# Counting whole turns of an angle in the low half of a float's word, with a new order of all operations

## The chip, the cores and the metric

The kernel runs on one core of one Trainium2 chip. The metric is the device time of one execution in microseconds. Three runs of the kernel before took 470.22, 471.32 and 486.15 us, so its time is the median, 471.32 us. The core has five engines that run side by side: PE (matmuls; PEld are its weight loads), DVE, ACT and POOL (elementwise work), and SP, which here only issues DMA transfers.

## The reference

A recurrence over 768 time steps feeds a small mixture of attention experts. The first part keeps a complex 48x48 state for each of 4 batches and 8 heads; each step multiplies row d of the state by a complex number of modulus at most 0.999 and adds `k v`:

```
mag = np.sqrt(a_re * a_re + a_im * a_im)
scale = np.minimum(mag, 0.999) / (mag + 1e-06)
a_re_n, a_im_n = (a_re * scale, a_im * scale)
for t in range(S):
    new_re = ar * S_re - ai * S_im
    new_im = ar * S_im + ai * S_re
    S_re, S_im = (new_re + kv, new_im)
    y[:, :, t] = np.einsum('bhd,bhde->bhe', q[:, :, t], S_re)
```

The second part takes `y` (4 x 768 x 384) as `x`. A gate `x @ w_gate` picks two of four experts for each token; each expert is causal attention with 64-wide projections, and the two outputs are summed with the gate's weights:

```
logits = x @ w_gate
q, k, v = x @ wq[e], x @ wk[e], x @ wv[e]
a = softmax(causal(scale * (q @ k.transpose(0, 2, 1))))
ye = a @ v @ wo[e]
out += mask[..., None] * w[:, :, kk:kk + 1] * ye
```

## The kernel before, in words

**The recurrence becomes matmuls.** The product of the complex factors up to step t is a modulus times a turn by an angle, so the kernel takes the logarithm of each modulus and the angle of each factor (`quotients`, `magnitudes`, `arcs`), sums both over time (scans on DVE), and multiplies `q` and `k` by the exponentials and by sine and cosine (`products`). With these, a chunk of 128 steps is plain linear attention: `head` transposes `k` on PE into tile pk and forms the scores psc, `state` adds a chunk's contribution pu to the running state tst, and `tail` adds the part within the chunk and the part from the state in tile yu, whose two halves (a rounded one and the rest) become `x`. In the trace a matmul on plain 32-bit floats stands as two instructions where the program has one.

**The angles** are the part that the change rewrites (function `angles`, lines 527 to 544). [...]

- "turns": `Bi` is scaled from radians to turns (ACT in batch 0, POOL in batches 1 to 3);
- the scan sums `Bi` along time into `A` (DVE);
- "wrap": `MAGIC`, 1.5 times two to the 23rd, is added to `A`, which rounds it to a whole number (POOL in all batches);
- a SCALAR_TENSOR_TENSOR on DVE takes `MAGIC` off again and subtracts `A`;
- "fold": the absolute value (ACT), for the cosine;
- `sines` takes both sines with a scale of minus 2 pi (ACT).

**Layout and stages.** The 384 rows (8 heads x 48) of a batch lie in three tiles j of 128 partitions (ab for the factors, qk for q and k). `regroup` sends them by DMA into tiles fm, one for each of four pairs of heads g, with 96 partitions. For g = 2 and 3 of batch 0 these have names of their own (fm2, fm3). Time is cut into three blocks k of 256 steps. Batch 0 is prepared in parts (`PARTS`): first j 0 at block 0, then j 1 and 2 at block 0, then blocks 1 and 2. Batch b + 1 is prepared while batch b is in the second part. For g = 3 the result yu goes to a tile yt and from there by six small DMAs into the three tiles x; every projection (tiles pp and pv) of a batch reads all three.

**What sets the order.** No engine order is found when the program is built. Every operation is recorded (4415 of them) and then issued in the order of a table, `ORDER`; each engine runs its own operations strictly in that order. A second table, `ROOMS`, picks the buffers. A third, `WARM`, puts matmuls on constants (tile src, line 380, 128x512 in bf16; their result, warm, is never read) on PE ahead of chosen operations: 242 in all, 151 of them at the start, 35 behind the first block of batch 0. All other instructions carry line 387.

Of the kernel before, what the change touches and what calls it, by code (L numbers as in the profile page):

```python
# [13 lines left out]
I32 = mybir.dt.int32  # L14
U8 = mybir.dt.uint8
AF = mybir.ActivationFunctionType
# [14 lines left out]
TWO_PI = 6.2831845  # L31
# [359 lines left out]
def attention_moe(ctx: ExitStack, tc: tile.TileContext, ak, vk, w, out):  # L391
# [154 lines left out]
    def sines(b, j, k0, k1):  # L546
        A, Bi, X, Y, Q, K, G, G2 = views(b, j, k0, k1)
        act(Bi, Bi, AF.Sin, scale=-TWO_PI)
        act(A, A, AF.Sin, scale=-TWO_PI, bias=halfpi)

# [413 lines left out]
```

## Time and profile before

| | |
|---|---|
| median of three runs | 471.32 us |
| the profiled execution, its time | 474.05 us |
| the profiled execution, its span from the first to the last instruction | 472.3 us |
| PE busy, share of the span | 453.0 us, 96% |
| DVE, ACT, POOL busy | 335.7, 328.7, 236.0 us |
| mean granted clock of PE | 0.949 of full speed |
| matmuls on constants, busy time on PE | 58.5 us, 242 of them |

The profiled execution is 2.73 us above the median. A busy PE isn't PE at its peak: in some stretches the throttle grants it half of its 2.4 GHz, and the same matmuls then take twice as long. The column PEclk of the tables by stretch shows this.

### The profile page before, as it was taken

Reading aid. Unit: us, or ns where it says so; the run is one execution under the profiler, and the core shown is the slowest. Engines: PE = TensorE matmul, PEld = TensorE weight load, DVE = VectorE, ACT = ScalarE, POOL = GpSimd, SP = SyncE. Lnnn points to the kernel's source line nnn. Section 1 sums busy time; section 2 is a strip of 40 time slices with the busy share of each in tenths; the row PEclk is TensorE's granted clock in tenths of the full one; section 3 lists DMA queues with packets and bytes.
Section 4 is the critical chain, followed back from the end, with each engine's and each line's share of the span. In section 5 each row is a group of like instructions: output and inputs, shape, how many; then the busy total and the mean of one; then the engine's idle time right before and its main releaser. Section 6 shows DMA issues by size and latency. Waiting matters only on the chain.

```text
span 472.3 us, 9992 instructions
## 1 busy us (share of the span) xinstructions
PE 453.0 (96%) x3754; PEld 350.8 (74%) x3754; DVE 335.7 (71%) x768; ACT 328.7 (70%) x731; POOL 236.0 (50%) x214
## 2 busy tenths in 40 slices
PE   8998999999998999998999999999999999999896
PEld 3447868778686678867988877788798787887565
DVE  3977548778789899774999895878965543666622
ACT  6984387976559979876789988768755565324453
POOL 4264054544424689587235697394224518003780
PEclk9997599979969999999999999999959999999999
DMA  7905067702973562365085813580445111100102
GB/s 274 348 3 134 1 160 198 207 19 77 237 206 67 168 194 78 87 176 158 4 199 129 234 46 102 117 236 18 76 112 139 30 25 29 51 18 17 52 1 101
DMA packets 22239, 53.46 MB, mean 113 GB/s; under 512 B 3216, under 2 KB 9456, under 8 KB 22064
## 3 DMA queue, kind: packets, MB, share of 16 engines
q1 hardware_dynamic: 22192, 52.83, 40.9%
q8 instruction: 29, 0.48, 0.4%
q14 instruction: 18, 0.15, 0.1%
HBM read 26.74 MB, written 4.72 MB: 67 GB/s over the span
## 4 chain that ended last, share of the span: by engine, by line
PE 58%; ACT 15%; DMA 9%; DVE 5%; POOL 5%; SPq 4%; issue 3%; POOLq 0%; ACTq 0%; DVEq 0%
PE pp L387 8%; PE psc L387 8%; PE yu L387 7%; PE psS L387 7%; PE pw L387 5%; ACT qk L387 5%; PE pv L387 5%; PE pu L387 5%; DMA fm<-qk 4%; ACT ab L387 4%; PE po L387 4%; SPq L387 4%; PE pm L387 3%; PE pk L387 3%; DMA ab<-in_ak_dram 3%
## 5 line engine op out<-in xcount | busy, mean ns | idle before, releaser
L387 POOL TENSOR_TENSOR pe<-pe 128x512 f32<-128x512 f32 (+1 forms) x64 | 83.9, 1311 | 16.7 <-PE po L387 13.3
L387 ACT ACTIVATE pe<-psS 128x512 f32<-128x512 f32 (+2 forms) x96 | 47.9, 540 | 22.2 <-PE psS L387 19.3
L387 ACT ACTIVATE ab<-ab 128x768 f32<-128x768 f32 (+2 forms) x81 | 55.6, 695 | 9.3 <-DVE ab L387 5.3
L387 PE MATMUL psc<-fm 96*128 96x128 f32 x384 | 60.5, 312 | 1.1 <-DVE sum L387 0.4
L380 PE MATMUL warm<-src 128*128 128x512 bf16 x242 | 58.5, 397 | 1.4 <-POOL src L387 1.4
L387 ACT ACTIVATE qk<-qk 128x768 f32<-128x768 f32 (+5 forms) x105 | 57.4, 563 | 1.1 <-DVE qk L387 0.7
L387 PEld LDWEIGHTS psc<-fm 96*128 96x128 f32 x384 | 54.4, 220 | 3.9 <-issue 0.9
L387 DVE CUSTOM_DVE_ANT_0 pm<-pm,mask 128x384 f32<-128x384 f32 (+4 forms) x96 | 47.2, 511 | 12.3 <-PE pm L387 11.8
L387 POOL TENSOR_SCALAR_AFFINE_SELECT pe<-pe 128x256 f32<-128x256 f32 x48 | 22.7, 485 | 63.6 <-ACT pe L387 31.3
L387 POOL TENSOR_TENSOR qk<-qk 128x768 f32<-128x768 f32 (+2 forms) x24 | 36.7, 1542 | 32.8 <-ACT qk L387 30.8
L387 PE MATMUL pp<-x,whi 128*128 128x256 f32 (+1 forms) x216 | 46.6, 328 | 3.6 <-ACT ob L387 2.0
L387 POOL TENSOR_TENSOR qk<-qk,ab 128x768 f32<-128x768 f32 (+2 forms) x19 | 28.7, 1510 | 39.4 <-ACT ab L387 20.9
L387 PE MATMUL psS<-qka 64*128 64x256 f32 (+3 forms) x480 | 47.4, 304 | 0.3
L380 PEld LDWEIGHTS <-src 128*128 128x128 bf16 x242 | 23.6, 102 | 31.0 <-issue 6.1
L387 ACT ACTIVATE tst<-sum,fm 96x48 f32<-96x48 f32 x128 | 38.3, 326 | 11.3 <-DVE sum L387 11.1
L387 DVE TENSOR_TENSOR pts<-psc,keep 128x512 f32<-128x512 f32 x48 | 32.8, 683 | 17.5 <-PE psc L387 15.3
L387 DVE TENSOR_TENSOR qk<-qk,ab 128x768 f32<-128x768 f32 (+2 forms) x41 | 38.5, 960 | 9.3 <-ACT ab L387 8.0
L387 PE MATMUL po<-pe,v 128*64 128x256 f32 (+3 forms) x320 | 44.3, 395 | 0.0
L387 PEld LDWEIGHTS psS<-qka 64*128 64x128 f32 x480 | 36.9, 185 | 7.7 <-issue 3.6
L387 PE MATMUL yu<-pts,vt 128*64 128x128 f32 x384 | 41.0, 309 | 0.4
L387 POOL TENSOR_SCALAR ab<-ab 128x768 f32<-128x768 f32 (+2 forms) x24 | 22.3, 931 | 37.0 <-DVE ab L387 19.0
L387 PEld LDWEIGHTS pp<-x,whi 128*128 128x128 f32 x216 | 33.2, 188 | 9.7 <-ACT ob L387 2.2
(106 smaller groups left out, 984.8 us busy)
## 6 DMA issues: line engine op xcount, KB each, us to landing
fm<-qk SPq DMA_DIRECT2D x18, 578.2 KB, 7.6
ab<-in_ak_dram SPq DMA_DIRECT2D x9, 768.0 KB, 7.2
qk<-in_ak_dram SPq DMA_DIRECT2D x9, 768.0 KB, 5.0
vt<-in_vk_dram SPq DMA_DIRECT2D x16, 384.0 KB, 8.4
out_dram<-ob SPq DMA_DIRECT2D x24, 192.0 KB, 1.9
fm<-qk SPq DMA_DIRECT2D x10, 385.5 KB
fm<-qk SPq DMA_DIRECT2D x16, 192.8 KB, 3.8
x<-yt SPq DMA_DIRECT2D x72, 32.0 KB, 2.0
```

Source lines behind the costliest of these rows:

```text
L380: chain("tensor", nc.tensor.matmul(x, *map(real, self.warm), start=True, stop=True))
L387: chain(engine, getattr(getattr(nc, engine), method)(*map(real, a), **{x: real(y) for x, y in k.items()}))
```

## The change

It has two parts. The first is in `angles` and `sines`. The angle stays in radians through the scan, so the operation "turns" is gone (15 of them: 6 on ACT in batch 0, 9 on POOL later). "Wrap" now multiplies the running angle by 1 / (2 pi) and adds `MAGIC` in one operation; in batch 0 it moves from POOL to ACT, 6 operations. After that addition the low 16 bits of the float's word hold the whole number of turns, and DVE reads them as 16-bit integers, every second one, multiplies by minus 2 pi and adds the angle. The result is within half a turn in radians, and both sines need hardly a scale.

```
-        if ENG0["turns"][k0][j] == "a" if b == 0 else ENG["turns"] == "a":
-            act(Bi, Bi, AF.Copy, scale=0.5 / math.pi)
-        else:
-            e("turns").tensor_scalar(Bi, Bi, 0.5 / math.pi, 0.0, op0=OP.mult, op1=OP.add)
         n = (k1 - k0) * C2
         nc.vector.tensor_tensor_scan(A, ones.to_broadcast([128, n]), Bi, carry[b, j] if k0 else 0.0, op0=OP.mult, op1=OP.add)
...
-        e("wrap").tensor_scalar(Bi, A, 1.0, MAGIC, op0=OP.mult, op1=OP.add)
-        nc.vector.scalar_tensor_tensor(Bi, Bi, MAGIC, A, op0=OP.subtract, op1=OP.subtract)
+
+        if (ENG0["wrap"][k0][j] if b == 0 else ENG["wrap"]) == "a":
+            act(Bi, A, AF.Copy, scale=0.5 / math.pi, bias=MAGIC)
+        else:
+            e("wrap").tensor_scalar(Bi, A, 0.5 / math.pi, MAGIC, op0=OP.mult, op1=OP.add)
+        nc.vector.scalar_tensor_tensor(Bi, Bi.bitcast(I16)[:, ::2], -TWO_PI, A, op0=OP.mult, op1=OP.add)
...
-        act(Bi, Bi, AF.Sin, scale=-TWO_PI)
-        act(A, A, AF.Sin, scale=-TWO_PI, bias=halfpi)
+        act(Bi, Bi, AF.Sin, scale=NEAR_ONE)
+        act(A, A, AF.Sin, scale=-NEAR_ONE, bias=halfpi)
...
-        "turns": ("aaa", "aaa", "aaa"), "wrap": ("ppp", "ppp", "ppp"), "fold": ("aaa", "aaa", "aaa")}
+        "wrap": ("aaa", "aaa", "aaa"), "fold": ("aaa", "aaa", "aaa")}
```

The second part is new tables: `ORDER` (4400 operations), `ROOMS`, and `WARM`, which now holds 205 matmuls on constants in place of 242 (the number stands second in each entry):

```
-    72: ("psu_4", 151), 1080: ("psu_4", 35), 390: ("psa_1", 8), 410: ("psu_4", 2), 420: ("psa_0", 3), 540: ("psu_4", 2), 1147: ("psa_2", 11),
-    1287: ("psa_2", 5), 1180: ("psa_2", 3), 840: ("psu_2", 4), 843: ("psu_1", 4), 1298: ("psu_4", 1), 1345: ("psa_1", 5), 1406: ("psu_0", 2),
-    4381: ("psa_1", 3), 4387: ("psa_1", 3),
+    71: ("psu_4", 146), 1234: ("psu_4", 18), 354: ("psa_2", 1), 1245: ("psa_2", 11), 693: ("psa_2", 2), 779: ("psu_3", 6), 1304: ("psu_2", 5),
+    1336: ("psu_0", 9), 4366: ("psa_0", 4), 4372: ("psa_0", 3),
```

The tables move instructions on every engine; three places matter here. The first is POOL at the start, in the preparation of block 0 of batch 0, where the row TENSOR_SCALAR on ab is "wrap" and TENSOR_TENSOR of qk with ab is `products`. Before:

```order
L387 TENSOR_TENSOR qk<-qk 128x256
L387 TENSOR_TENSOR qk<-qk 128x2x256
L387 TENSOR_SCALAR ab<-ab 128x256 x2
L387 TENSOR_TENSOR qk<-qk,ab 128x256 x2
L387 TENSOR_SCALAR ab<-ab 128x256
L387 TENSOR_TENSOR qk<-qk,ab 128x256 x2
```

And now:

```order
L387 TENSOR_TENSOR ab<-ab 128x512 x2
L387 TENSOR_TENSOR qk<-qk 128x256 x3
L387 TENSOR_TENSOR qk<-qk,ab 128x256 x4
L387 TENSOR_SCALAR qk<-qk 128x2x256
L387 TENSOR_TENSOR qk<-qk,ab 128x256
```

The three "wrap" rows are gone from POOL, and the products follow each other. The second place is PE at the end of block 0 of batch 0. Before, fm_423 is the tile of g = 2 and fm_466 that of g = 3:

```order
L387 MATMUL psc<-fm_466 128x128 x4
L387 MATMUL yu<-pts,vt 64x128 x4
L387 MATMUL yu<-fm_423,tst 48x128 x2
L387 MATMUL pu<-vt,kts 96x48 x4
L387 MATMUL yu<-pts,vt 64x128 x4
L387 MATMUL yu<-fm_466,tst 48x128 x2
L380 LDWEIGHTS src
```

Now fm_252 is g = 2 and fm_426 is g = 3:

```order
L387 MATMUL psc<-fm_426 128x128 x4
L387 MATMUL pu<-vt,kts 96x48 x4
L387 MATMUL yu<-pts,vt 64x128 x4
L387 MATMUL yu<-fm_426,tst 48x128 x2
L387 MATMUL pu<-vt,kts 96x48 x4
L387 MATMUL yu<-pts,vt 64x128 x4
L387 MATMUL yu<-fm_252,tst 48x128 x2
L380 LDWEIGHTS src
```

The yu of g = 3, whose result goes to x by DMA, now stands ahead of pu and yu of g = 2, and not last. Behind it stood 35 matmuls on constants, and now 18. On SP the six transfers x<-yt now follow each other; before, a load of qk stood between the fourth and the fifth. The third place is DVE in batch 2, where the three products of tile j = 1 of batch 3 (qk with ab, 128x3x256) stand among the row maxima (pm, mx) and residues (qka) of batch 2. Before:

```order
L387 ISA pm,mx<-pm,mask 128x384
L387 ISA mx 128x1
L387 TENSOR_TENSOR qka<-pp,qka 128x256
L387 TENSOR_TENSOR qk<-qk,ab 128x3x256 x3
L387 TENSOR_REDUCE mx<-pm 128x1
L387 ISA pm,mx<-pm,mask 128x384
```

And now:

```order
L387 ISA pm,mx<-pm,mask 128x128
L387 ISA mx 128x1
L387 TENSOR_TENSOR qk<-qk,ab 128x3x256
L387 TENSOR_TENSOR ot<-r,ot 128x256
L387 TENSOR_TENSOR qk<-qk,ab 128x3x256
L387 TENSOR_TENSOR sum<-tst,pu 96x96
L387 TENSOR_TENSOR qka<-pp,qka 128x256 x4
L387 TENSOR_TENSOR qk<-qk,ab 128x3x256
```

Two of the three now stand ahead of four residues and behind another row maximum.

## Rows read from the trace of the kernel before

**Rows 1.** The page, part 1: busy us (share of the span) x instructions.

```profile
PE 453.0 (96%) x3754; PEld 350.8 (74%) x3754; DVE 335.7 (71%) x768; ACT 328.7 (70%) x731; POOL 236.0 (50%) x214
```

**Rows 2.** Table by stretch: start:end, length, PE, PEld, DVE, ACT, POOL busy, PEclk, DMA.

```profile
38.00:58.40 20.40, 19.94 (x129) 17.87 (x130) 14.16 (x23) 6.76 (x20) 5.22 (x5) 0.56 0.23 57
58.40:67.00 8.60, 8.60 (x38) 3.71 (x36) 5.86 (x8) 7.57 (x20) 4.64 (x4) 0.86 0.48 126
80.60:98.20 17.60, 16.52 (x158) 12.86 (x157) 14.41 (x35) 17.05 (x40) 7.41 (x5) 1.00 0.61 182
98.20:105.20 7.00, 6.99 (x36) 5.94 (x36) 4.47 (x14) 5.17 (x9) 5.08 (x4) 0.51 0.12 25
129.00:139.20 10.20, 10.20 (x62) 9.43 (x61) 8.06 (x19) 6.18 (x15) 2.91 (x2) 0.50 0.87 243
344.00:354.40 10.40, 10.40 (x66) 9.62 (x64) 6.48 (x19) 5.67 (x15) 2.49 (x1) 0.51 0.45 112
```

**Rows 3.** PE in time, 28 to 39 us: start, us, what, idle before it.

```profile
27.69 8.80 PE L380 MATMUL warm<-src 128*128 128x512 bf16 x40
38.18 0.27 PE L387 MATMUL pk<-ident,fm 96*128 96x96 f32 x1 [1.69 <-DMA fm<-qk]
38.73 0.47 PE L387 MATMUL pk<-ident,fm 96*128 96x96 f32 x3 [0.28 <-DMA fm<-qk]
```

**Rows 4.** ACT in time, at 11 and 27 us.

```profile
11.15 0.61 ACT L387 ACTIVATE qk<-ab 128x512 f32<-128x512 f32 x1
11.67 0.40 ACT L387 ACTIVATE ab<-ab 128x256 f32<-128x256 f32 x1
...
27.18 1.28 ACT L385 ACT_TABLE_LOAD   x1
```

**Rows 5.** DVE, POOL and SP in time, 29 to 35 us.

```profile
29.37 0.69 DVE L387 TENSOR_TENSOR_SCAN ab<-col,ab 128x256 f32<-128x256 f32 x1 [1.39 <-ACT ab L387]
...
30.15 0.49 POOL L387 TENSOR_SCALAR ab<-ab 128x256 f32<-128x256 f32 x1 [1.22 <-DVE ab L387]
...
34.64 1.34 SPq L387 DMA_DIRECT2D fm<-qk  x2
```

**Rows 6.** PE and SP in time, 55 to 67 us.

```profile
55.44 1.52 PE L387 MATMUL pu<-vt,kts 128*96 128x48 f32 x8
...
58.37 8.90 PE L380 MATMUL warm<-src 128*128 128x512 bf16 x35
66.92 0.47 PE L387 MATMUL pv<-whi,x 128*128 128x260 f32 x1
...
59.38 2.57 SPq L387 DMA_DIRECT2D x<-yt  x4
62.00 0.58 SPq L387 DMA_DIRECT2D qk<-in_ak_dram  x1
62.63 1.22 SPq L387 DMA_DIRECT2D x<-yt  x2
```

**Rows 7.** The page, part 6: transfers, KB each, median us from issue to landing.

```profile
x<-yt SPq DMA_DIRECT2D x72, 32.0 KB, 2.0
```

**Rows 8.** Groups by form, whole span: count, busy us, mean ns, idle before.

```profile
L387 POOL TENSOR_SCALAR ab<-ab 128x768 f32<-128x768 f32 x18 | 18.4, 1028 | 24.2 <-ACT ab L387 14.5 <-DVE ab L387 7.3 <-DVE lg L387 1.9
L387 DVE SCALAR_TENSOR_TENSOR ab<-ab 128x768 f32<-128x768 f32 x9 | 9.1, 1017 | 1.2 <-POOL ab L387 1.2
```

**Rows 9.** DVE and PE in time, at 333 and 343 us.

```profile
332.76 2.69 DVE L387 TENSOR_TENSOR qk<-qk,ab 128x768 f32<-128x768 f32 x3
...
342.64 0.47 PE L387 MATMUL pk<-ident,fm 96*128 96x96 f32 x3 [1.16 <-DMA fm<-qk]
```

**Rows 10.** PE in time, 78 to 95 us.

```profile
80.66 0.55 PE L387 MATMUL pk<-ident,fm 96*128 96x96 f32 x4
...
86.88 0.83 PE L387 MATMUL pk<-ident,fm 96*128 96x96 f32 x4
...
94.29 0.60 PE L380 MATMUL warm<-src 128*128 128x512 bf16 x2
```

More of the change, by code (lines that the diff above doesn't have):

```diff
@@ L14 @@
 I32 = mybir.dt.int32
+I16 = mybir.dt.int16
 U8 = mybir.dt.uint8
@@ L30 @@
 MAGIC = 1.5 * 2.0 ** 23
-TWO_PI = 6.2831845
+TWO_PI = 2.0 * math.pi
+NEAR_ONE = 1.0 - 2.0 ** -23
 NEG = -1.0e9
@@ L47 @@
 ORDER = [
[184 rows of a table removed]
[183 rows of a table added]
 ]
 ROOMS = [
[22 rows of a table removed]
[22 rows of a table added]
 ]
 WARM = {
-    72: ("psu_4", 151), 1080: ("psu_4", 35), 390: ("psa_1", 8), 410: ("psu_4", 2), 420: ("psa_0", 3), 540: ("psu_4", 2), 1147: ("psa_2", 11),
-    1287: ("psa_2", 5), 1180: ("psa_2", 3), 840: ("psu_2", 4), 843: ("psu_1", 4), 1298: ("psu_4", 1), 1345: ("psa_1", 5), 1406: ("psu_0", 2),
-    4381: ("psa_1", 3), 4387: ("psa_1", 3),
+    71: ("psu_4", 146), 1234: ("psu_4", 18), 354: ("psa_2", 1), 1245: ("psa_2", 11), 693: ("psa_2", 2), 779: ("psu_3", 6), 1304: ("psu_2", 5),
+    1336: ("psu_0", 9), 4366: ("psa_0", 4), 4372: ("psa_0", 3),
 }
 ENG = {"inv_m": "d", "exp_q": "p", "kts": "a", "xh": "a", "pp": "a", "pv": "a", "first": "p", "inv_a": "p",
-       "exp_k": "p", "q_sin": "d", "k_sin": "p", "q_cos": "d", "k_cos": "d", "turns": "p", "wrap": "p", "fold": "a",
+       "exp_k": "p", "q_sin": "d", "k_sin": "p", "q_cos": "d", "k_cos": "d", "wrap": "p", "fold": "a",
        "sum": "p", "oth": "a", "otl": "d"}
```

411 rows, old and new, of tables (ORDER, ROOMS) are left out of this document.

## The prediction

> **What bounds the kernel now.** I read the page's table of engines first: PE is busy for 453.0 of 472.3 us [rows 1], DVE, ACT and POOL for 50 to 71%. So an operation that leaves POOL or ACT gives nothing by itself; it counts only where PE waits for it or fills a wait with matmuls on constants. The 3754 PE instructions hold 242 of these, 58.5 us, and with 19.3 us of idle time that is what an order can win, besides the clock.
>
> Next comes the table by stretch, for the clock [rows 2]. Four stretches run at the lower of the two levels, 1.2 GHz: most of 38 to 61 us (0.56, then 0.86 for the stretch in which it rises), 98.2 to 105.2, 129 to 139.2 and 344 to 354.4, together about 21 + 7 + 10 + 10 = 48 us. PE is never idle in them, so each costs about half its length. All hold the small matmuls of the recurrence (pk, psc, pu, yu). The reader is to see that busy time hides this loss.
>
> Then the waits and the time-ordered views. At the start PE runs constants until 36.49, waits 1.69 and 0.28 us for the first tile fm, and falls to half clock about 2 us later [rows 3]. Behind block 0, 35 constants bridge the way of yt into x [rows 6]. Until 342.64 PE waits 1.16 us for an fm tile of batch 3 [rows 9], and the clock falls some 1.5 us later.
>
> The profiled execution took 474.05 us, 472.3 of span and 1.75 around it, 2.73 us or 0.6% above the median of 471.32. I make the sum against the former and take the difference off the latter.
>
> **The change part by part.**
>
> *The angles by themselves: nothing.* 9 "turns" leave POOL at about 1.03 us [rows 8], 9.2 us; 6 "wraps" of 0.5 to 0.8 us leave it too. ACT in batch 0 loses 6 operations and gains 6 of the same shapes. PE's work covers all of it; POOL is idle half the span. Without that cover, a turn and a handoff on the way to each fm tile, some 1 us, would count, as at the start.
>
> *The 16-bit, every-second read.* No row shows one. The nearest is the same instruction on 32-bit floats, 1.017 us at 128x768 [rows 8]. From below, 16 bits could not save more than the 0.5 us that half of it is, from above I allow as much again. Fifteen of them lie beside PE work, three on the way to the first tile: 0, ends of minus and plus 0.2 us (half of 0.40 us, its time at 128x256).
>
> *The first fm tile: minus 1.4 us.* Ahead of the sine table's load on ACT, at 27.18, stand two 512-wide operations and one tiny copy fewer than before. One takes 0.52 us from start to start [rows 4], so 1.1 us. On the way from the arc to the scan one operation, 0.3 us, is gone. The "wrap" (0.49 us on POOL [rows 5]) becomes one of about 0.4 on ACT without a handoff to POOL and back. From the scan (29.37) to the transfer's issue (34.64) it takes 5.27 us; going through the new order by hand I get 4.1. So the tile comes between 1.1 and 2.4 us earlier. The 5 fewer constants make 5 x 0.216 (8.80 us less the last one's 0.38, over 39 steps [rows 3]) = 1.1 us. I take 1.1 + 0.3, nearest the smaller end, because the later one of tile and constants sets the start; ends minus 1.1 and minus 2.4.
>
> *The end of block 0: minus 3.1 us.* PE ends the block at 58.37, and six transfers with a load between them leave SP until 63.85; with 2.0 us to land [rows 6, 7] x is there at 65.9, and the projection starts at 66.92. In the new order, yu of g = 3 stands ahead of pu and yu of g = 2, which take 58.37 - 55.44 = 2.9 us at half clock, and the load (0.58) is behind the transfers. So x is there 65.9 - 58.37 - 2.9 - 0.6 = 4.0 us after the block's end. Of the 35 constants, some 7 ran at half clock in the first 3.0 us; 18 would take 3.0 + 11 x 0.216 = 5.4 us where 35 took 8.55. That is 3.1 less, and x still comes first. Ends: 0, if x comes late all the same, and minus 4.5 if the clock is up and x itself sets the start. The next fm tiles are issued behind these six transfers, so they gain as much and the gain isn't given back there.
>
> *The other constants: minus 2.5 us.* From there to the middle of batch 0's attention stood 50, and now 34; at the end 6, and now 7. 15 x 0.216 = 3.2 us if the data are there, 0 if each becomes a wait. I take most of it, as the tiles come 4.5 us earlier and PE reaches them as much earlier.
>
> *Batch 3's tile j = 1: minus 0.6 us.* Its three products start at 332.76, behind a row maximum that waits for PE, and end 335.45; the transfers are issued at once, and PE waits for them from 341.48 [rows 9]. Now two products stand ahead of four residues and the third behind them. This may close the wait of 1.16 us or not; I take half. If it goes, the tile j = 2, whose products come later on the same engine, is the next that can be late.
>
> Sum: -1.4 - 3.1 - 2.5 - 0.6 = -7.6 us: 466.4 against the 474.05, **463.7 us** against the median.
>
> **A rule against it.** The clock stayed up from 80.6 to 98.2 us although pk, psc, pu and yu fill that stretch; 7 constants stand inside it and 8 right ahead of it [rows 2, 10], and the fall came 4 us after the last two. At the start and in batch 3 the falls come about 2 us after the first rows of pk that follow a wait [rows 3, 9]. So in this trace transposes and their company go with falls, constants with a held clock. The Trainium skill, page "TensorE: Matmul & The Clock Gate", Part 4, says that a transpose doesn't count as busy PE time in the same way and doesn't bring the full clock. The trace agrees where it shows falls, but not that every pk costs the clock. By that rule the new order, with one constant in that stretch for 15, would lose the clock there, which is the second rival below.
>
> **The rivals.**
>
> 1. *The half clock shrinks too: 455 us, between the two cases below, chance 0.25.* If the wait at 341.48 closes, the stretch of 10.4 us behind it may go, 5.2 us, and the rest of the wait, 0.6: 463.7 - 5.8 = 458. A second of these stretches (10.2 or 7.0 us [rows 2]) gives 3.5 to 5.1 more, 453 to 454. For it: two of four falls follow a wait for fm. Against: the others don't, and the first stretch, the longest, has the same matmuls in the same density as before.
>
> 2. *The clock falls in block 1 and stays down: 479 us, chance 0.14.* The matmuls of 80.6 to 98.2 take 16.52 us, less 7 x 0.216 for constants: 15.0 us; at half clock they take as much again, 471.3 - 7.6 + 15.0 = 478.7. It decides once 7.6 us of that matmul time, about half, run at half clock: beyond it the kernel is slower than before. For it: the constants that are gone there, and that one of three runs before took 486.15. Against: 18 constants and 5 us of dense 128x128 projections still lead into it, with fewer holes.
>
> 3. *Constants become waits: 469 us, chance 0.18.* If the tiles come no earlier than they did, PE idles where the 32 constants behind the start stood, and only the start's 1.4 and part of the rest remain: 471.3 - 2 to 3. For it: the fill is only as good as the order's guess; before, the guess for the first tile was 1.69 us short. A form of it is that the change doesn't do what it says: it speaks of more matmuls on constants, and the table has 205 for 242. The sum goes by the table.
>
> **How the numbers follow.** Forecast 0.43 (459 to 467), rivals 0.25, 0.14 and 0.18. The predicted time is the forecast's, 464. Two per cent, 9.4 us, is about what a measurement of this kernel can tell from no change: faster lies below 461.9, slower above 480.7. Below 461.9 lies rival 1 with a third of the forecast, 0.39; above 480.7, where the second stretch of recurrence (129 us) is lost longer as well, half of rival 2, 0.07; the rest is 0.54. The range 452 to 476 leaves out the far fifth of rival 1, 0.05, and two thirds of rival 2, 0.09, and takes in the ends of all terms (together from 470.4 down to 459.8).
>
> **What would show each step.** Right: the first pk at 36 to 37 us; the projection about 5 us behind the end of block 0, with no wait ahead of it, and 4 to 5 us earlier than 66.92; pk of block 1 without a wait for fm; PE busy about 445 us with constants at 50. Wrong: waits of 1 us and more on fm or x right behind the constants (rival 3); a PEclk of 0.5 between 65 and 95 us (rival 2); SCALAR_TENSOR_TENSOR on ab far from 1.0 us. The forecast fails most easily by the clock, since one stretch of 10 us at half clock more or less is worth more than any of my terms.

## The result and the profile after

The changed kernel took 450.79 us, median of four runs (450.36 to 456.27); the kernel before 470.77 in the same session. The ratio is 0.962, 95% interval 0.952 to 0.972. The forecast was 464, the range 452 to 476: the direction is right, the size is not. The time fell by 20 us where the sum had 7.6, and the median lies 1.2 us below the range.

Ratios are taken over runs within 1.5% of a kernel's fastest, and since what differs from run to run is here TensorE's clock itself, I also give the median of all runs and the lowest and highest mean granted clock among them.

The table of engines, answering to [rows 1]:

```profile
PE 425.3 (95%) x3708; PEld 332.9 (74%) x3717; DVE 336.4 (75%) x768; ACT 327.5 (73%) x731; POOL 224.6 (50%) x199
```

PE is busy 27.7 us less and idle 4 us more (23.3 for 19.3). The matmuls on constants account for 12.8 of it: 45.7 us for 58.5, with 196 of the 205 in the trace. The rest, 14.9 us, fits the clock. The mean granted clock is 0.984 for 0.949; one minus this, times the span, is what I call the time lost, 7.2 us for 24.1, so 16.9 us less. The row of the clock in forty slices, and the table by stretch (columns as in [rows 2]), show where it is still lost:

```profile
PEclk9997899999999999999999999999999999999999
```

```profile
37.80:48.70 10.90, 10.89 (x64) 10.25 (x64) 7.17 (x12) 5.89 (x15) 4.04 (x3) 0.53 0.39 97
48.70:55.40 6.70, 6.08 (x66) 4.86 (x66) 6.47 (x10) 5.47 (x15) 0.63 (x1) 1.00 0.03 7
65.30:98.00 32.70, 29.68 (x293) 24.67 (x294) 25.70 (x59) 28.52 (x68) 15.59 (x12) 1.00 0.65 181
98.00:106.00 8.00, 7.75 (x55) 5.98 (x55) 7.66 (x17) 4.96 (x11) 4.24 (x3) 1.00 0.15 43
116.00:130.00 14.00, 13.64 (x128) 10.76 (x128) 13.21 (x37) 12.27 (x29) 3.29 (x2) 1.00 0.84 217
144.00:150.00 6.00, 5.51 (x27) 2.53 (x27) 4.65 (x8) 5.85 (x11) 2.87 (x4) 0.72 0.15 33
330.00:344.00 14.00, 14.00 (x172) 12.04 (x173) 9.38 (x30) 9.62 (x26) 5.76 (x8) 1.00 0.68 156
```

Of the four half-clock stretches of [rows 2] the last three are gone, and block 0 runs slow until 48.5 us, not 61. One short dip (a stretch at half clock) near 144 us is new. PE in time at the places of [rows 3] and [rows 6]:

```profile
37.81 0.52 PE L387 MATMUL pk<-ident,fm 96*128 96x96 f32 x4 [3.42 <-DMA fm<-qk]
...
55.47 3.83 PE L380 MATMUL warm<-src 128*128 128x512 bf16 x17 [0.16 <-issue]
58.95 0.58 PE L387 MATMUL pp<-x,whi 128*128 128x256 f32 x2
...
72.62 0.69 PE L387 MATMUL pk<-ident,fm 96*128 96x96 f32 x6 [1.09 <-DMA fm<-qk]
...
144.43 1.98 PE L387 MATMUL po<-pe,v 128*64 128x512 f32 x4 [2.97 <-POOL pe L387]
```

The first pk starts 0.37 us earlier than before, behind a longer wait, and its four instructions now follow without a second one. The projection starts 3.6 us behind the end of block 0 (55.31) where it took 8.55. Two new waits stand at 72 and 144 us (po is the attention's weights times v).

### The profile page after: what moved, and what is told of

Read it like the earlier page. It is cut to its first block, busy times and chain, and to the rows that moved or that the text cites. A ratio compares the mean times of both kernels' runs of the same rounds, so it can differ in the third digit from the quotient of the medians.

```text
span 448.6 us, 9894 instructions
## 1 busy us (share of the span) xinstructions
PE 425.3 (95%) x3708; PEld 332.9 (74%) x3717; DVE 336.4 (75%) x768; ACT 327.5 (73%) x731; POOL 224.6 (50%) x199
## 4 chain that ended last, share of the span: by engine, by line
PE 52%; DMA 7%; POOL 3%; SPq 3%; DVE 3%; ACT 2%; issue 1%; POOLq 0%; ACTq 0%; DVEq 0%
PE psS L387 9%; PE pp L387 8%; PE po L387 7%; PE yu L387 6%; PE pw L387 5%; PE psc L387 4%; DMA fm<-qk 4%; PE pv L387 4%; SPq L387 3%; PE pu L387 3%; PE pm L387 2%; POOL pe L387 2%; PE dn L387 2%; PE pk L387 2%; DMA qk<-in_ak_dram 1%; DVE qk L387 1%
## 5 line engine op out<-in xcount | busy, mean ns | idle before, releaser
L387 POOL TENSOR_TENSOR pe<-pe 128x512 f32<-128x512 f32 (+1 forms) x64 | 82.5, 1290 | 19.5 <-PE po L387 14.5
L387 PE MATMUL psc<-fm 96*128 96x128 f32 x384 | 53.9, 289 | 0.4 <-ACT kts L387 0.2
L387 POOL TENSOR_TENSOR qk<-qk,ab 128x768 f32<-128x768 f32 (+2 forms) x19 | 29.9, 1578 | 42.3 <-ACT ab L387 30.3
L387 PEld LDWEIGHTS psc<-fm 96*128 96x128 f32 x384 | 48.7, 200 | 2.8 <-ACT kts L387 1.0
L387 PE MATMUL po<-pe,v 128*64 128x256 f32 (+3 forms) x320 | 45.7, 401 | 3.0 <-POOL pe L387 3.0
L380 PE MATMUL warm<-src 128*128 128x512 bf16 x196 | 45.7, 388 | 2.1 <-POOL src L387 1.4
L387 PE MATMUL pp<-x,whi 128*128 128x256 f32 (+1 forms) x216 | 45.6, 327 | 2.1 <-ACT pe L387 1.4
L380 PEld LDWEIGHTS <-src 128*128 128x128 bf16 x205 | 19.8, 100 | 25.6 <-issue 2.9
L387 PE MATMUL yu<-pts,vt 128*64 128x128 f32 x384 | 37.5, 286 | 1.1 <-DVE pts L387 0.7
L387 PE MATMUL pu<-vt,kts 128*96 128x48 f32 x320 | 35.8, 252 | 0.8 <-DVE sum L387 0.4
```

Source lines behind the costliest of these rows:

```text
L380: chain("tensor", nc.tensor.matmul(x, *map(real, self.warm), start=True, stop=True))
L387: chain(engine, getattr(getattr(nc, engine), method)(*map(real, a), **{x: real(y) for x, y in k.items()}))
```

## The experiments

Line numbers in the rows of some kernels differ by a few, since their tables have other lengths. The median and the range of mean clocks stand behind each. The runs fall into three sessions: the first four kernels, the next four, the last four. The kernel before, run in each, had medians of 473.83, 471.85 and 470.82 us.

**The angles alone, on the old order.** The changed kernel with the order, buffers and constants of before (less the 15 turns), and the wraps of batch 0 on POOL as there:

```
-         "wrap": ("aaa", "aaa", "aaa"), "fold": ("aaa", "aaa", "aaa")}
+         "wrap": ("ppp", "ppp", "ppp"), "fold": ("aaa", "aaa", "aaa")}
```

> The changed arithmetic of the angles (15 turns gone, whole turns from the low half of the word) in the order of before, with the wraps of batch 0 left on POOL and the constants of before. Theory 1 (the gain is the order's alone, the angles are hidden): within 2 us of before, 469 to 472 us, and the four half-clock stretches of before stay, mean granted clock near 0.95. Theory 2 (shorter chains on POOL and ACT close the waits, and with them the falls of the clock): 455 to 463 us, no wait of 1 us for fm at 342 us.

468.07 us (clock 0.948 to 0.980), before 473.83 in that session, ratio 0.983 (0.974 to 0.992). At the same mean clock of 0.967 this kernel took 467.3 and 468.85, the one before 466.65, 470.4 and 471.85: no difference that can be told. What the median gained is clock, and theory 1 on the angles stands as to time. Not all four stretches stayed, though: in its profile the first two fall as in before, the last two don't. The wait ahead of batch 3's pk is there, and the clock holds behind it:

```profile
340.39 0.47 PE L394 MATMUL pk<-ident,fm 96*128 96x96 f32 x3 [1.16 <-DMA fm<-qk]
```

```profile
340.40:350.40 10.00, 10.00 (x110) 9.17 (x111) 9.29 (x29) 8.47 (x22) 3.15 (x2) 1.00 0.51 114
```

**The order alone, with the old angles.** Order, buffers and constants of the change, and the arithmetic of before; each turn stands right behind its arc, a place I chose:

```
+        if ENG0["turns"][k0][j] == "a" if b == 0 else ENG["turns"] == "a":
+            act(Bi, Bi, AF.Copy, scale=0.5 / math.pi)
+        else:
+            e("turns").tensor_scalar(Bi, Bi, 0.5 / math.pi, 0.0, op0=OP.mult, op1=OP.add)
...
-         "wrap": ("aaa", "aaa", "aaa"), "fold": ("aaa", "aaa", "aaa")}
+         "turns": ("aaa", "aaa", "aaa"), "wrap": ("ppp", "ppp", "ppp"), "fold": ("aaa", "aaa", "aaa")}
```

> The order, buffers and constants of the change with the old arithmetic of the angles: each turn stands right behind its arc, on ACT in batch 0 and on POOL later; the wraps of batch 0 are on POOL. Theory 1 (order alone): 450 to 453 us, clock 0.98, one half-clock stretch at 38 to 49 us. Theory 2 (angles matter through the waits): 457 us or more, with waits for fm of 1 us and more in batches 1 to 3 and a clock below 0.97.

469.71 us (0.945 to 0.963), ratio 0.987 (0.977 to 0.996): theory 2. PE in time, then the stretch behind the second wait:

```profile
38.76 0.52 PE L392 MATMUL pk<-ident,fm 96*128 96x96 f32 x4 [3.00 <-DVE qk L392]
...
77.25 0.69 PE L392 MATMUL pk<-ident,fm 96*128 96x96 f32 x6 [2.27 <-DMA fm<-qk]
```

```profile
78.50:112.70 34.20, 34.20 (x198) 29.01 (x193) 18.39 (x43) 23.19 (x50) 12.72 (x10) 0.50 0.37 113
```

The turns make the first pk 0.95 us later and the wait at the same matmuls as at 72.62 in the changed kernel 1.2 us longer. Behind the second wait PE ran 34.2 us at half clock, 17.1 us lost, in the one profile taken. The half clock need not be all of it: at mean clocks of 0.960 and 0.963 two other runs took 469.71 and 465.43, where the change, in a later session, took 452.97 at 0.968. Where those microseconds went, no profile shows. So the angles are hidden on the old order, and are not on the new one.

**The start filled.**

```
-    71: ("psu_4", 146), ...
+    71: ("psu_4", 162), ...
```

> The changed kernel with 162 constants ahead of the first pk for 146: 16 x 0.216 = 3.5 us of matmuls where PE waited 3.42 us for the first tile. Theory A (the wait of 3.42 us costs the clock of block 0): the clock holds or falls for a short time only, block 0 ends 3 to 5 us earlier, 446 to 448 us. Theory B (block 0's small matmuls lose the clock whatever stands ahead of them): half clock again from about 39 to 48 us, 450.5 to 451.5 us.

449.60 us (0.951 to 0.996), ratio 0.946 (0.935 to 0.956). PE in time and the table by stretch:

```profile
37.83 0.49 PE L394 MATMUL pk<-ident,fm 96*128 96x96 f32 x4
...
51.93 4.06 PE L387 MATMUL warm<-src 128*128 128x512 bf16 x18
...
68.91 0.89 PE L394 MATMUL pk<-ident,fm 96*128 96x96 f32 x6 [1.06 <-DMA fm<-qk]
```

```profile
37.80:51.90 14.10, 12.09 (x129) 10.42 (x127) 13.23 (x21) 10.61 (x28) 4.08 (x4) 1.00 0.32 78
69.20:79.50 10.30, 10.30 (x63) 8.33 (x62) 4.75 (x10) 7.08 (x14) 5.12 (x4) 0.50 0.75 203
```

The first pk starts when it did, without a wait, and block 0 keeps the full clock and ends 3.4 us earlier. That is what theory A expects of this place, in one profile; the time stays above the 446 to 448 it gave. In this run the clock then fell behind the next wait for fm, at 68.9, which it had survived in the profile of the change.

**Six constants in before's wait of batch 3.**

```
+    2945: ("psa_2", 6),
```

> The kernel before with six constants (6 x 0.216 = 1.3 us) ahead of the pk of batch 3 that waited 1.16 us for its tile until 342.64. Theory A (a PE wait ahead of the recurrence costs the clock): the half-clock stretch of 344 to 354 us is gone, 5 us less, 465 to 467 us. Theory B (the recurrence without other matmuls loses it): the stretch stays, 470 to 471 us.

470.38 us (0.935 to 0.992), ratio 0.979 (0.967 to 0.990). The profile fell in a run with much half clock elsewhere. PE in time at this place, and the stretch:

```profile
353.36 1.47 PE L385 MATMUL warm<-src 128*128 128x512 bf16 x6
354.89 0.75 PE L392 MATMUL pk<-ident,fm 96*128 96x96 f32 x4
```

```profile
354.90:366.00 11.10, 11.10 (x124) 10.13 (x125) 9.95 (x32) 9.22 (x24) 3.72 (x3) 1.00 0.52 117
```

The wait is filled and the stretch that ran at 0.51 in [rows 2] runs at 1.00. That does not show that the fill did it: in the profiles of the angles alone (above) and of the eighteen on the old order (below) the wait is there, 1.16 and 1.14 us, and the clock is 1.00 behind it too. Nor does the time decide, which missed theory A's 465 to 467: the other stretches vary from run to run by more than these 5 us.

**The small groups of constants taken out of the change.**

```
-    354: ("psa_2", 1), 1245: ("psa_2", 11), 693: ("psa_2", 2), 779: ("psu_3", 6), 1304: ("psu_2", 5), 1336: ("psu_0", 9),
```

> The changed kernel without the six small groups of constants behind block 0 (1, 11, 2, 6, 5 and 9, together 34, 7.3 us); the 146, the 18 and the 7 at the end stay. Theory A (they fill waits that are there anyway, and keep the clock through them): spans at equal clock within 1 us of the changed kernel's, but more half-clock stretches, a mean clock below 0.97 and 455 to 462 us. Theory B (the clock does not hang on them): 448 to 451 us, clock 0.977 to 0.984. Theory C (filler that delays work): 444 us.

461.93 us (0.923 to 0.973) in ten runs, ratio 0.982 (0.961 to 1.004): theory A. 34 constants, 7.3 us of work that computes nothing, are worth 9 to 11 us against the change's two medians (452.97 and 450.79), which are from other sessions. PE's longest waits in its profile, us in total, times, longest:

```profile
PE po L394 <- POOL pe L394: 3.9, 1, 3.9
PE pk L394 <- DMA fm<-qk: 3.9, 2, 3.2
```

**Eighteen constants behind block 0 on the old order.**

```
-    72: ("psu_4", 151), 1080: ("psu_4", 35), ...
+    72: ("psu_4", 151), 1080: ("psu_4", 18), ...
```

> The kernel before with 18 constants behind block 0 for 35, nothing else. My step on the end of block 0 holds that the new order of g = 3 and g = 2 is what makes the shorter fill possible: here x lands some 7.5 us behind the block's end, the constants last 5.4 us, so PE waits about 2 us for x and the projection starts 1.0 us earlier than in before: -1 us, or +1 to +5 where the clock falls behind that wait. Rival (the 35 were simply too many): no wait for x, -3.7 us.

466.52 us (0.960 to 0.974), before 471.85; ratio 1.011 (0.992 to 1.029), set against the two fastest runs of before, 459.87 and 465.09 at clocks of 0.996 and 0.977. PE and SP in time:

```profile
52.01 4.06 PE L385 MATMUL warm<-src 128*128 128x512 bf16 x18
57.36 0.36 PE L392 MATMUL pv<-whi,x 128*128 128x260 f32 x1 [1.29 <-DMA x<-yt]
60.77 0.51 PE L392 MATMUL pv<-whi,x 128*128 128x260 f32 x2 [3.05 <-DMA x<-yt]
...
55.90 0.58 SPq L392 DMA_DIRECT2D qk<-in_ak_dram  x1
56.53 1.22 SPq L392 DMA_DIRECT2D x<-yt  x2
```

x lands when it did, 8.8 us behind the block's end, and PE waits 4.3 us for it. The shorter fill alone saves nothing there; the new order is what brings x earlier. Part of that is the load of qk ahead of the last two transfers. By the times at which the trace has them land, these two took 3.75 and 3.57 us here and 3.63 and 3.64 in before; in the change, where no load stands between the six, 1.95 and 1.98. Moving the load alone was not tried. Also to be seen: in this run block 0 kept the full clock although PE had waited 1.42 us for its first tile.

**The start and the wait at 72 us filled.**

```
-    71: ("psu_4", 146), 1234: ("psu_4", 18), 354: ("psa_2", 1), ...
+    71: ("psu_4", 162), 1234: ("psu_4", 18), 354: ("psa_2", 1), 503: ("psa_0", 5), ...
```

> The changed kernel with 162 constants at the start and 5 more (1.08 us) ahead of the pk of g = 1, k = 2 in batch 0, where PE waited 1.06 to 1.09 us for fm in both earlier profiles. Theory A (falls of the clock come behind PE waits that stand ahead of the recurrence): the only half-clock stretch left is the 3.4 us at 144, clock 0.99 or more in nearly all runs, 445 to 447 us. Theory B (falls come by the mix of matmuls, wherever a wait was): clocks scatter as with 162 alone, 0.95 to 0.996, median near 449.5 us.

446.47 us, six runs of 444.30 to 447.35 with clocks of 0.996 to 1.000; ratio 0.965 (0.957 to 0.972), again against those two runs, while the median of before was 471.85. Theory A: no run fell out, and in the profile only the dip near 144 is left, here from 142.1. This is the fastest version measured, and I call it the best version.

```profile
67.56 1.25 PE L387 MATMUL warm<-src 128*128 128x512 bf16 x5
68.88 0.71 PE L394 MATMUL pk<-ident,fm 96*128 96x96 f32 x6
```

**The mask ahead of the quotient on POOL**, on top of that kernel:

```
-    ... 1690, 675, 1688, 823, 844, 845, 683, 1299, 1691, 685, 1304, 1305, 824, 676, 684, 1349, ...
+    ... 675, 1688, 823, 844, 845, 683, 1299, 1690, 685, 1304, 1305, 824, 676, 684, 1691, 1349, ...
```

1690 is the quotient of batch 2 and 1299 the mask, both on POOL; 1691 is the quotient's arc and 684 the second sine of batch 1, on ACT.

> The kernel with 162 and 5 more constants, and on POOL the causal mask of the first score block in batch 0 ahead of the quotient of batch 2 (2.52 us), with that tile's arc behind the two sines on ACT. Theory A: the wait of 2.97 us of the first po ahead of 144 us falls to about 0.5 us and with it the 3.4 us at half clock: 2 to 4 us less than the kernel without this edit, 442 to 444 us. Rival (the arc's delay comes back as a wait of psS for ACT's exponentials a few us later): within 1 us of that kernel.

447.91 us (0.988 to 1.000), ratio 0.970 (0.960 to 0.980): the rival, though 1.4 us above that kernel and not within 1. The wait of po is gone, waits of 1.6 us for DVE and of 1.4 of psS (the attention's scores) for ACT took its place, and a dip of 3.4 us came all the same, at 146.1.

**That wait filled instead.**

```
-    1304: ("psu_2", 5), ...
+    1304: ("psu_2", 18), ...
```

> The kernel with 162 and 5 more constants, and 18 ahead of the first po of batch 0 for 5: 13 x 0.216 = 2.8 us where PE waited 2.97 us for POOL's mask. Theory A (a wait of PE ahead of small matmuls is what loses the clock): the last half-clock stretch, 3.4 us behind that wait, is gone, the mean clock is 1.000 and the time 1 to 2 us below that of the kernel without this edit, 444.5 to 446 us. Theory B (no link with the wait): the stretch stays, 446.5 us; if the 18 outlast the mask, up to 0.5 us more.

448.67 us (445.49 to 452.86, clock 0.989 to 1.000), ratio 0.954 (0.950 to 0.959). In the profile the dip is gone: po starts without a wait behind the constants, and the mean clock is 1.000.

```profile
141.63 1.08 PE L394 MATMUL po<-pe,v 128*64 128x512 f32 x4
```

But the times scatter more than those of the kernel without the edit, in the session before, and their median is not lower. Whether this fill is worth anything stays open.

**The change once more.** No edit.

> The changed kernel once more, to set its runs beside those of the kernel with 162 and 5 more constants. Theory A: half-clock time varies from run to run, 5 to 20 us, and the time with it by 0.7 to 0.9 us for each us lost to the clock; median 450 to 453 us. Theory B (the clock of 0.977 to 0.984 was typical, the rest chance): all runs within 449.5 to 451.5 us.

452.97 us (450.80 to 463.82, clock 0.944 to 0.989), ratio 0.964 (0.960 to 0.969): theory A on the scatter, though one us of lost clock is not one price. The profiled run lost 10.2 us, all in block 0, and took 450.80; the first profile of the change lost 7.2 and took 450.36; a run at 0.968 took the same 452.97 as one at 0.973.

PE and the table by stretch:

```profile
37.40 0.52 PE L387 MATMUL pk<-ident,fm 96*128 96x96 f32 x4 [2.06 <-DMA fm<-qk]
```

```profile
40.20:60.60 20.40, 19.59 (x112) 16.13 (x114) 14.12 (x24) 11.63 (x28) 3.96 (x3) 0.50 0.17 43
```

So the rise at 48.5 us in the first profile was no property of the new order, and the first pk alone differs by 0.41 us between two profiles of one program.

**Three waits of before filled.**

```
-    72: ("psu_4", 151), ...
+    72: ("psu_4", 160), 702: ("psa_2", 3), 2945: ("psa_2", 6), ...
```

> The kernel before with constants in three of its PE waits: 160 for 151 at the start (wait of 1.97 us in all), 3 ahead of the first pk of batch 1 (0.65 us ahead of 127 us) and 6 ahead of the pk of batch 3 (1.16 us). If the work and the clock are two separate parts of the gain: the clock comes to 0.98 or more in most runs, and the time to 460 to 464 us, about half of the change's gain, while the other 10 to 13 us need the new order. Rival (the gain is the clock alone): 450 to 455 us. Rival (constants don't hold it): 468 to 472 us.

462.09 us (458.98 to 463.82, clock 0.989 to 1.000), ratio 0.983 (0.979 to 0.987). Eighteen constants give the old order half of what the change gives, and the rest stays out of reach, as expected if work and clock are two parts. PE in time:

```profile
52.70 7.50 PE L385 MATMUL warm<-src 128*128 128x512 bf16 x34 [0.16 <-issue]
59.85 0.47 PE L392 MATMUL pv<-whi,x 128*128 128x260 f32 x1
61.29 0.50 PE L392 MATMUL pv<-whi,x 128*128 128x260 f32 x2 [0.97 <-DMA x<-yt]
...
208.01 0.62 PE L392 MATMUL pp<-x,whi 128*128 128x256 f32 x3 [2.11 <-ACT ob L392]
...
283.94 0.60 PE L392 MATMUL pv<-whi,x 128*128 128x260 f32 x2 [1.39 <-DMA x<-yt]
```

**The wraps of batch 0 back on POOL**, in the changed kernel:

```
-         "wrap": ("aaa", "aaa", "aaa"), "fold": ("aaa", "aaa", "aaa")}
+         "wrap": ("ppp", "ppp", "ppp"), "fold": ("aaa", "aaa", "aaa")}
```

> The changed kernel with the wraps of batch 0 on POOL for ACT; the arithmetic stays new. My term for the first tile says that a wrap on ACT saves the handoff to POOL and back: first pk 0.3 to 0.6 us later than 37.8, the tiles behind it up to 1 us later, 451 to 453 us at a clock of 0.98. Rival (the DMA's landing, not the angles, sets the tile): first pk at 37.8, time unchanged at 450 to 451 us.

454.86 us (0.962 to 0.983), ratio 0.968 (0.963 to 0.974), beside 452.97 of the change.

```profile
37.90 0.52 PE L387 MATMUL pk<-ident,fm 96*128 96x96 f32 x4 [3.36 <-DMA fm<-qk]
...
72.81 1.19 PE L387 MATMUL pk<-ident,fm 96*128 96x96 f32 x6 [1.56 <-DMA fm<-qk]
...
28.57 0.69 DVE L387 TENSOR_TENSOR_SCAN ab<-col,ab 128x256 f32<-128x256 f32 x1 [0.29 <-ACT ab L387]
33.64 0.70 SPq L387 DMA_DIRECT2D fm<-qk  x1
```

```profile
72.70:89.70 17.00, 16.89 (x100) 14.50 (x100) 8.18 (x18) 10.42 (x20) 9.12 (x7) 0.50 0.53 150
```

The first pk is 0.09 us later than in the first profile of the change and 0.50 later than in the second, so by that time alone neither side can be told. The way from the scan to the first transfer's issue can: 5.07 us here, where the change took 4.64 (29.02 to 33.66) and 4.63 in its second profile. So the wrap on ACT saves 0.43 us there, as the term said, and the rival is wrong at this place. The difference of 1.9 us in the medians lies within the scatter of the clock.

## Why the forecast was right in direction and wrong in size

**The gain has two parts.** They come apart where the clock is nearly full in both orders. The two runs of the filled kernel before with clocks of 0.999 and 1.000 took 459.46 and 458.98 us. The three runs of the best version at 0.999 and 1.000 took 446.73, 446.39 and 444.30. The difference of the medians, 459.2 and 446.4, is 12.8 us: this is the work and its order, since the constants added to either fill waits. The two are from different sessions, but in that of the filled kernel before, the kernel with 18 ahead of po took 445.49 and 446.68 at 1.000, which comes to the same. The other 7 to 8 of the 20 us are clock. Over 41 runs of the kernel before in these sessions the clock ran from 0.925 to 0.996 and the time from 486.30 to 459.87, 0.77 us for each us lost.

**The step that failed: the half clock.** The prediction saw that three of its four stretches cost 3.5 to 5.2 us each and the first about 10. It put their shrinking at 0.25, as rival 1, with one or two gone, because "the others don't" follow a wait for fm and the first stretch "has the same matmuls in the same density as before". In the change's first profile all four shrank or went, in its second all but the first went. The prediction had also missed that a third fall, at 129.0, came behind a wait, for DVE and not for fm; with it stand two waits of before that are read further down:

```profile
126.66 0.51 PE L387 MATMUL pm<-qka 64*128 64x384 f32 x2 [0.65 <-DVE qka L387]
...
218.74 0.50 PE L387 MATMUL pp<-x,whi 128*128 128x256 f32 x2 [1.98 <-ACT ob L387]
...
292.57 0.51 PE L387 MATMUL pv<-whi,x 128*128 128x260 f32 x2 [0.89 <-DMA x<-yt]
```

The runs show why the argument on density was poor: density did not decide. The old order's block 0 ran at half clock for 20 us in the profile of [rows 2] and at full clock in that of the kernel with 18 constants behind it; the change's ran slow for 10 us in one profile and for 20 in the other. What moved the odds was constants in the waits ahead of the recurrence: they brought the mean clock from 0.944 to 0.989 in ten runs of the change to 0.988 to 1.000 in the 18 runs of the best version and its two variants, and from 0.925 to 0.996 to 0.989 to 1.000 on the old order, and taking out 34 constants brought it down to 0.923 to 0.973. A fill both closes a wait and adds dense matmuls; which of the two holds the clock, no run separates. And it is odds and no law: PE waited 1.09 us at 72.62 in the change and the clock held, and in before it fell at 98.2 with only 0.22 us of waiting just ahead.

**Rival 2, the fall in block 1,** did not come in either profile of the change: the clock is 1.00 from 65.3 to 98 us, with one constant in that stretch. The rule of the Trainium skill, page "TensorE: Matmul & The Clock Gate", Part 4, that a transpose does not bring the full clock therefore did not decide here. But the danger was real: behind the wait for fm in that block three other kernels fell for 10.3, 17.0 and 34.2 us (162 at the start, the wraps on POOL, the old angles). The same page of the Trainium skill, Part 1, says that a busy PE comes to full clock; in the row of 78.5 to 112.7 above the profile has PE busy without a gap and the clock stays at 0.50, so by that measure the trace disagrees. How full the array was in that stretch, the profile doesn't show.

**The terms of the sum**, against the runs at nearly full clock where these show them:

- *The angles, 0:* right on the old order. On the new order the old angles cost waits and clock; the prediction had warned that without PE's cover some 1 us would count.
- *The 16-bit read, 0, ends of plus and minus 0.2:* right. At 256 and 512 elements it takes 0.408 and 0.675 us for 0.410 and 0.680 in 32 bits. At 768 the mean in the change is 0.19 us longer, 1.205 for the 1.017 of [rows 8], but on the old order the same read (last line) takes 0.974, so the new order's neighbours make it longer and not the read.

```profile
L387 DVE SCALAR_TENSOR_TENSOR ab<-ab 128x768 f32<-128x768 int16 x9 | 10.8, 1205 | 1.1 <-POOL ab L387 0.9
...
L387 DVE SCALAR_TENSOR_TENSOR ab<-ab 128x512 f32<-128x512 int16 x3 | 2.0, 675 | 0.0
L387 DVE SCALAR_TENSOR_TENSOR ab<-ab 128x256 f32<-128x256 int16 x3 | 1.2, 408 | 0.0
...
L394 DVE SCALAR_TENSOR_TENSOR ab<-ab 128x768 f32<-128x768 int16 x9 | 8.8, 974 | 1.3 <-POOL ab L394 1.3
```

- *The first tile, minus 1.4:* about minus 1.0 in this pair of profiles, though the first pk moved by 0.37 alone. ACT, DVE and SP in time, answering to [rows 4, 5]; the last line is of before:

```profile
26.97 1.28 ACT L385 ACT_TABLE_LOAD   x1
...
29.02 0.69 DVE L387 TENSOR_TENSOR_SCAN ab<-col,ab 128x256 f32<-128x256 f32 x1 [0.30 <-ACT ab L387]
...
33.66 1.99 SPq L387 DMA_DIRECT2D fm<-qk  x3
...
34.64 2.15 SPq L387 DMA_DIRECT2D fm<-qk  x3
```

The table load moved by 0.21 us, not 1.1: counting operations ahead of it was not reading what ACT waits for. From the scan to the issue it takes 4.64 us; I had 4.1. The issue is 0.98 us earlier. Two of the three transfers that leave together carry what pk needs. In before the first pk waits for the first of them and the second pk, at 38.73, for the second; now the first pk already waits for the second transfer, as the semaphores in the trace show. That one lands at 37.67 for 38.69, 1.02 us earlier, some 3.3 us behind its issue in both. So nothing is lost on the way; the two first pk wait for different things. One pair of profiles is not the last word either: over the seven profiles with the change's angles and order the issue stands at 32.55 to 33.66, over the four with both old at 34.44 to 35.24.

- *The end of block 0, minus 3.1:* the step is right, the size nearer its far end, minus 4.5. With the clock up in both, the projection starts 7.15 us behind the constants' start in the filled kernel before (52.70 to 59.85) and 3.70 in the best version (51.72 to 55.42): minus 3.4. But there the old order still waits 0.97 us for x, at 61.29, so minus 4.4 in all. The prediction had x land at 65.9 in before, with 2.0 us for each transfer; the trace has it at 66.90, since the two behind the load took 3.6. So the load's place, which the sum gives 0.6, may be worth some 2.2.
- *The other constants, minus 2.5:* less than 1. From block 0's end to the first pk of block 1 the two kernels differ by 4.2 us (13.93 for 9.68), which the term above uses up; up to the first dn (the sums under the softmax), in batch 0's attention, the whole lead is 5.7 us (161.40 and 155.68). Dropping constants is no gain by itself, as the run without the small groups shows.
- *Batch 3's tile, minus 0.6:* right, the wait is gone. Whether the clock behind it went with the wait is not shown, since it held in two kernels that have the wait.

So 5.7 us of lead in batch 0, where the sum had 7.0; the best version's dip at 142.1, 1.7 us lost, lies ahead of that dn and can account for the difference. The lead at the last dn is 16.0 us (450.15 and 434.15), in two profiles at clocks of 0.993 and 0.996. **The second thing missed** is these 10 us in batches 1 to 3, for which I had 0.6. The lead grows by 4.5 us around the wait of pp for ACT at 208, and by 4.3 around the waits near 284; either place has a half-clock dip of 1.7 us in the filled kernel before, so some 7 of the 10 are work and waits. In the profile before the same waits are 1.98 us at 218.74 and 0.89 at 292.57. No run closed them alone. I had read PE's waits only at the start, behind block 0 and where the clock fell.

**Rival 3, constants become waits,** was half right: the start's wait grew from 1.97 to 3.42 us in the first profile (2.06 in the second) and two more came, yet PE's idle time grew by 4 us only.

## What to carry to other kernels

Where PE waits ahead of small matmuls, price the wait by the clock that may go with it (5.1 us behind one of 1.06, 17.1 behind one of 2.27, nothing behind one of 1.09), and take a clock that varies from run to run as a distribution: compare kernels at the same mean clock before giving a gain to an edit. Fill such waits with matmuls on constants first, since 21 of them took the change from 452.97 to 446.47 us (in two sessions), and 18 gave the old order half of the change's gain. Before you compare two waits, see whether they wait for the same transfer. When an order is rewritten as a whole, list every PE wait of the old one, in all stages, and ask of each whether the new order closes it.

## What the runs showed that I had not expected

- The same program loses from run to run anything from 2 to 36 us to the clock (span times one minus the mean clock, 41 runs of the kernel before), and a single profile shows one draw of that.
- A PE that the profile has busy without a gap can stay at the lower level for 34.2 us, with 198 matmuls of the recurrence and its neighbours in it.
- A transfer of 32 KB landed 2.0 us behind its issue, and 3.6 to 4.0 us behind it with a load of 768 KB issued just ahead, in three profiles of the old order. That the load is the cause was not tried alone.
